# Attention and routed experts on one core: the last 64 key positions of the probabilities are transposed a turn later, inside the score tiles

## The chip, the cores and the metric

The kernel runs on one core of a Trainium2 chip. The time is device microseconds (us) from one launch, and fewer is better. A core has TensorE (PE in the profile, with its weight loads as PEld), VectorE (DVE), ScalarE (ACT), GpSimd (POOL) and SyncE (SP, which issues loads). They work side by side, each in the order in which its own instructions stand, and wait for each other through semaphores.

## What is computed

```python
def _attn_ref(q, k, v, tau):              # q, k, v: 8 batches x 8 heads x 576 x 64
    scores = q @ k.T / sqrt(64)
    scores = where(scores >= max(scores) - tau, scores, -1e9)
    attn = exp(scores - max(scores))
    attn = attn / (sum(attn) + 1e-9)
    return attn @ v

def _moe_ref(x, w_gate, w_output_gate, w1, w2):   # x: 4608 x 512, 8 experts of 1024
    e_idx = argmax(x @ w_gate)
    gate_w = softmax(x @ w_gate)[e_idx]
    eom = 1 / (1 + exp(-(x @ w_output_gate)))
    for e in range(8):
        mask = e_idx == e
        out[mask] = gate_w * eom[:, e] * (relu(x[mask] @ w1[e]) @ w2[e])
```

The attention output of all heads, put side by side, is the `x` of the experts. The change touches the attention alone.

## The kernel before, in words

The attention works in 32 units, each a pair of batches at one head. The two batches lie on the two halves of the 128 partitions. A unit has five turns `t` = 0 to 4 over the query rows: turns 0 to 3 take 128 queries of each batch (so two score tiles of 128 x 576), turn 4 takes the last 64 queries of both batches in one tile. `Attention.run` writes out the order of all engines by hand, turn after turn (`g` counts the turns of all units), and the scheduler is told to keep it on PE, DVE and ACT. A turn `g` works on several units of work at once:

- **scores** (L113 to L143): the score matmuls of turn `g` go to one or two `ps` tiles in PSUM, 1024 columns wide (two banks), of which columns 224 to 800 are used; columns 0 to 224 are free. DVE reads a `ps` tile with a running minimum and leaves `s` (L137). The pool has two `ps` tiles, so turn `g + 1` overwrites those of turn `g`.
- **x_rows** (L242 to L252, in turn 4 alone): small matmuls turn the unit before's output into rows, in the tiles `pr` and `pa`; ACT copies them out (L312).
- **exps** (L145 to L150): ACT makes `p` = exp(`s`), one instruction for each tile.
- **av_units** (L211 to L229): the product with `v` for the unit before, spread over turns 0 to 3 by the table `AV`. It reads the transposed probabilities `PTa` (turns 0 and 1 of its unit) and `PTb` (turns 2 to 4); its first matmuls of each half read block 8, the one that holds the last 64 key positions of both batches (the "remainder"). ACT copies the sums out (L228).
- **blocks** (L185 to L194): 16 transposes of `p` of turn `g - 2` to the tile `pt`, which ACT copies to `PTa` or `PTb` (L194). There is one `pt`. For a turn 4 it is **last_block** (L196 to L209) instead.
- **masks** (L152 to L166): DVE applies the threshold to `p` of turn `g - 1`.

The remainder of a turn's `p` has its own function, **remainder** (L168 to L183). In most turns it is two matmuls against the identity, 64 rows of `p` columns wide and 128 columns long, to a `pr` tile (L182), and one ACT copy (L183), right ahead of `blocks` and for the same turn `g - 2`:

```python
for pp in hs:
    o = M + pp.start
    nc.tensor.matmul(pr[pp, 0:P], p[:, o : o + 64], self.ident, start=True, stop=True)
nc.scalar.copy(PT[:, RB, q0 : q0 + P], pr[:, 0:P])
```

In a turn 4 that has `x_rows` it is a "pair" instead: two transposes of 64 rows (L177), one for each half of the queries, into columns of `pr` and `pa` that `x_rows` leaves free, and two ACT copies of 64 columns (L178).

Of the kernel before, what the change touches and what calls it, by code (L numbers as in the profile page):

```python
# [8 lines left out]
F32 = mybir.dt.float32  # L9
# [7 lines left out]
P = 128  # L17
# [3 lines left out]
class Attention:  # L21
    WU = 7
    SB = 4
    PB = 3
    LB = 3
    VB = 4
    WARM = {0: 4, 1: 2}
# [85 lines left out]
        self.load_qk(1)  # L113
        self.load_v(1)

    def scores(self, u, t):
        nc = self.nc
        q, k = self.loaded[u][0:2]
        S, HS = self.S, self.HS
        c0 = 512 - HS  # L120
        n = 2 if t < self.NB else 1
        ps = [self.ps_s.tile([P, 1024], F32, name="ps") for _ in range(n)]
        qs = q[:, t * P : t * P + P]
        for hf in range(2):
            for a in range(n):
                k0 = 0 if a else self.R
                pp = self.half[a] if n == 2 else slice(0, P)
                nc.tensor.matmul(  # L128
                    ps[a][:, c0 + hf * HS : c0 + hf * HS + HS], qs[pp], k[pp, k0 + hf * HS : k0 + hf * HS + HS],
                    start=True, stop=True,  # L130
                )
        mn = self.w3.tile([P, 2], F32, name="mn", bufs=4)
        ss = []
        SC = -(self.D ** -0.5)
        for a in range(n):
            s = self.sp.tile([P, S], F32, name="s", bufs=self.SB)
            nc.vector.tensor_scalar(  # L137
                s, ps[a][:, c0 : c0 + S], SC, None, op0=ALU.mult, op1=ALU.min, accum_out=mn[:, a : a + 1]
            )
            ss.append(s)  # L140
        thr = self.w3.tile([P, 2], F32, name="thr", bufs=4)
        self.router.gate = nc.gpsimd.tensor_scalar(thr[:, 0:n], mn[:, 0:n], self.tau, None, op0=ALU.add)  # L142
        return ss, mn, thr  # L143

    def exps(self, u, t, ss, mn, thr):  # L145
        p = self.sp.tile([P, 2 * self.S], F32, name="p", bufs=self.PB)
        for a, s in enumerate(ss):
            e = p[:, a * self.S : a * self.S + self.S]
            self.nc.scalar.activation(e, s, AF.Exp, bias=mn[:, a : a + 1], scale=-1.0)  # L149
        return p  # L150

    def masks(self, u, t, ss, mn, thr, p, between=None):  # L152
# [12 lines left out]
            nc.vector.tensor_copy(sums[:, 9:10], sums[:, 8:9])  # L165
            self.inverse(u)  # L166

    def remainder(self, u, t, p, pair=None):  # L168
        nc, hs, M, RB = self.nc, self.half, self.M, self.NK - 1
        if t == 0:  # L170
            self.PTa = self.w2.tile([P, self.NK, self.QA], F32, name="PTa")
        if t == 2:
            self.PTb = self.w2.tile([P, self.NK, self.S - self.QA], F32, name="PTb")
        PT, q0 = self.PTa if t < 2 else self.PTb, t % 2 * P
        if pair:
            for h in range(2):
                nc.tensor.transpose(pair[h], p[hs[h], M : M + P], self.ident[hs[h], hs[h]])  # L177
            return lambda h: nc.scalar.copy(PT[:, RB, q0 + 64 * h : q0 + 64 * h + 64], pair[h])  # L178
        pr = self.ps_r.tile([P, 512], F32, name="pr")
        for pp in hs:  # L180
            o = M + pp.start
            nc.tensor.matmul(pr[pp, 0:P], p[:, o : o + 64], self.ident, start=True, stop=True)  # L182
        nc.scalar.copy(PT[:, RB, q0 : q0 + P], pr[:, 0:P])  # L183

    def blocks(self, u, t, p):  # L185
        nc, id_, hs, RB = self.nc, self.ident, self.half, self.NK - 1
        PT, q0 = self.PTa if t < 2 else self.PTb, t % 2 * P
        pt = self.ps_t.tile([P, 1024], F32, name="pt")
        for b in range(RB):
            for h in range(2):  # L190
                o, k0 = h * 512 + b * 64, (b + b // 4) * P
                nc.tensor.transpose(pt[:, o : o + 64], p[hs[h], k0 : k0 + P], id_[hs[h], hs[h]])  # L192
        dst = PT[:, 0:RB, q0 : q0 + P].rearrange("p b (h j) -> p b h j", j=64)
        nc.scalar.copy(dst, pt.rearrange("p (h b j) -> p b h j", h=2, j=64))  # L194
# [93 lines left out]
    def run(self, hooks):  # L288
        nc, T, nu, rt = self.nc, self.NB + 1, self.nu, self.router
        G, W = nu * T, self.XW  # L290
        st, pr, av = {}, {}, {}
        self.prep_first()
        for g in range(G + T):
            u, t = divmod(g, T)
            if g < G:
                if t == 0 and u + 2 < nu:
                    self.load_qk(u + 2)
                    self.load_v(u + 2)
                st[g] = self.scores(u, t)
            if g in self.WARM:  # L300
                self.keep_warm(self.WARM[g])
            g2 = g - 2
            u2, t2 = divmod(g2, T)
            turn = 0 <= g2 < G
            xu = u - 1 if t == self.NB and u else None
            if xu is not None:
                ps = self.x_rows(xu)
                if turn:
                    out = self.remainder(u2, t2, pr[g2], [x[:, 5 * W : 5 * W + 64] for x in ps])
                xl = self.w2.tile([P, 2, 5, W], F32, name="xl")  # L310
                for a in (1, 0):
                    nc.scalar.copy(xl[:, a].rearrange("p j w -> p (j w)"), ps[a][:, 0 : 5 * W])  # L312
                    if turn:
                        out(a)
                self.x_out(xu, xl)
            if g < G:
                pr[g] = self.exps(u, t, *st[g])
            if t == 0 and u:
                av[u - 1] = self.av_units(u - 1)
            if u:  # L320
                for _ in range(*self.AV[t]):
                    next(av[u - 1])
            if turn:
                p = pr.pop(g2)
                if t2 == self.NB:
                    self.last_block(p)
                else:
                    if xu is None:
                        self.remainder(u2, t2, p)
                    self.blocks(u2, t2, p)  # L330
            if t == 1:
                rt.place(self.ps_r)
            g1 = g - 1
            if 0 <= g1 < G:
                self.masks(*divmod(g1, T), *st.pop(g1), pr[g1])
            if xu is not None:
                self.logits(xu, xl)
                if xu == nu - 1:
                    self.logit_sums(0)
                    self.logit_sums(1)  # L340
            if self.sumup and t in self.ROUTE:
                self.logit_sums(0 if t == self.ROUTE[0] else 1)
            if g in hooks:
                hooks[g]()
            rt.advance(t in self.ROUTE or u >= nu - self.H - 2)
# [301 lines left out]
class Experts:  # L647
    RB, NW, YB = 4, 4, 4
# [474 lines left out]
```

## Time and profile before

| what | value |
|---|---|
| median of 3 runs | 1011.85 us (1011.4 to 1012.84) |
| the profiled execution's own time | 1011.66 us |
| its span, first to last instruction | 1009.9 us |
| PE busy | 982.0 us (97% of the span) |
| DVE busy | 704.0 us (70%) |
| ACT busy | 604.5 us (60%) |
| POOL busy | 325.5 us (32%) |
| granted clock of TensorE, mean over the span | 0.993 |

The page's busy shares are means over two stages: the attention, to about 530 us, and the experts behind it. "Busy" of an instruction that is pipelined with its neighbours can be longer than the time by which it moves the next one, so the starts of neighbouring rows tell more than their durations. A weight load (PEld) is what waits on PE: a matmul's wait stands on its weight load.

### The profile page before, as it was taken

Reading aid. Unit: us, or ns where it says so; the run is one execution under the profiler, and the core shown is the slowest. Engines: PE = TensorE matmul, PEld = TensorE weight load, DVE = VectorE, ACT = ScalarE, POOL = GpSimd, SP = SyncE. Lnnn points to the kernel's source line nnn. Section 1 sums busy time; section 2 is a strip of 40 time slices with the busy share of each in tenths; the row PEclk is TensorE's granted clock in tenths of the full one; section 3 lists DMA queues with packets and bytes.
Section 4 is the critical chain, followed back from the end, with each engine's and each line's share of the span. In section 5 each row is a group of like instructions: output and inputs, shape, how many; then the busy total and the mean of one; then the engine's idle time right before and its main releaser. Section 6 shows DMA issues by size and latency. Waiting matters only on the chain. (4 is left out here: it accounts for less than half of the span.)

```text
span 1009.9 us, 21861 instructions
## 1 busy us (share of the span) xinstructions
PE 982.0 (97%) x8363; PEld 715.8 (71%) x8363; DVE 704.0 (70%) x1696; ACT 604.5 (60%) x1084; POOL 325.5 (32%) x617
## 2 busy tenths in 40 slices
PE   9999999999999999999989999999999999999894
PEld 5666666666666666666658888788878778778683
DVE  7898989899889998999876763435535436446621
ACT  6787887888887787778873432324424435336411
POOL 4344343454464556455536601102102002002101
PEclk9999999999999999999999999999999999999997
DMA  9962122121332114122216864335526526437201
GB/s 273 286 221 80 41 80 56 64 80 41 101 123 70 56 68 163 48 80 72 96 40 222 245 236 136 110 128 197 188 85 223 166 84 233 144 110 266 84 1 43
DMA packets 68843, 127.20 MB, mean 126 GB/s; under 512 B 6143, under 2 KB 32895, under 8 KB 68736
## 3 DMA queue, kind: packets, MB, share of 16 engines
q1 hardware_dynamic: 62096, 104.75, 33.0%
q0 software_dynamic: 6640, 21.02, 5.5%
q8 instruction: 67, 1.10, 0.5%
q14 instruction: 40, 0.33, 0.1%
HBM read 96.31 MB, written 30.22 MB: 125 GB/s over the span
## 5 line engine op out<-in xcount | busy, mean ns | idle before, releaser
L149 ACT ACTIVATE p<-s,mn 128x576 f32<-128x576 f32 x288 | 212.5, 783 | 53.8 <-DVE s L137 53.3
L137 DVE TENSOR_SCALAR_CACHE_REDUCE s<-ps 128x576 f32<-128x576 f32 x288 | 207.2, 752 | 36.2 <-PE ps L128 34.8
L159 DVE SCALAR_TENSOR_TENSOR p<-s,thr,p 128x576 f32<-128x576 f32 x288 | 225.3, 815 | 4.9 <-POOL thr L142 4.6
L128 PE MATMUL ps<-qk 64*128 64x288 f32 (+1 forms) x1152 | 198.7, 421 | 0.0
L907 ACT ACTIVATE hh<-ph 128x512 fp32r<-128x512 f32 (+2 forms) x96 | 48.8, 508 | 225.4 <-PE ph L904 219.5
L142 POOL TENSOR_SCALAR thr<-mn,tau_sb 128x2 f32<-128x2 f32 (+1 forms) x160 | 111.7, 698 | 214.1 <-DVE s L137 213.1
L908 DVE SCALAR_TENSOR_TENSOR hl<-ph,hh 128x512 fp32r<-128x512 f32 (+2 forms) x96 | 55.6, 579 | 164.5 <-ACT hh L907 162.0
L902 PE MATMUL ph<-xh,w1h 128*128 128x512 f32 (+2 forms) x384 | 136.5, 356 | 1.6 <-ACT xl L312 0.9
L903 PE MATMUL ph<-xl,w1h 128*128 128x512 f32 (+2 forms) x384 | 134.5, 350 | 3.0 <-DVE xl L732 2.2
L904 PE MATMUL ph<-xh,w1l 128*128 128x512 f32 (+2 forms) x384 | 133.4, 347 | 0.0
L128 PEld LDWEIGHTS ps<-qk 64*128 64x128 f32 (+1 forms) x1152 | 114.9, 189 | 22.1 <-DVE s L137 3.1
L720 POOL DMA_INDIRECT out_dram<-yo,kid x39 | 44.2, 1133 | 267.9 <-DVE yo L719 197.7
L926 PE MATMUL py<-w2h,hl 128*128 128x512 f32 x304 | 120.8, 397 | 1.0 <-DVE hl L908 1.0
L924 PE MATMUL py<-w2h,hh 128*128 128x512 f32 x304 | 120.5, 397 | 0.0
L925 PE MATMUL py<-w2l,hh 128*128 128x512 f32 x304 | 120.4, 396 | 0.0
L223 PE MATMUL pa<-PTb,vld 128*64 128x320 f32 x640 | 102.3, 447 | 1.0 <-ACT PTb L208 1.0
L192 PE MATMUL pt<-ident,p 64*128 64x64 f32 x2048 | 89.5, 227 | 3.6 <-ACT PTb L194 0.8
L192 PEld LDWEIGHTS pt<-ident,p 64*128 64x128 f32 x2048 | 73.6, 138 | 22.4 <-ACT PTb L194 10.8
L223 PE MATMUL pa<-PTa,vld 128*64 128x256 f32 x640 | 83.2, 389 | 0.3 <-ACT PTb L178 0.3
L903 PEld LDWEIGHTS ph<-xl,w1h 128*128 128x128 f32 x384 | 72.1, 188 | 15.8 <-DVE xl L732 6.0
L902 PEld LDWEIGHTS ph<-xh,w1h 128*128 128x128 f32 x384 | 72.1, 188 | 13.5 <-ACT xl L312 1.1
L732 DVE TENSOR_TENSOR w1l<-r,w1h 128x1024 fp32r<-128x1024 f32 x52 | 63.6, 1224 | 23.4 <-ACT w1h L729 22.9
(204 smaller groups left out, 1502.5 us busy)
## 6 DMA issues: line engine op xcount, KB each, us to landing
r<-in_moe_w_dram SPq DMA_DIRECT2D x104, 512.0 KB, 3.6
qk<-in_qkv_dram SPq DMA_DIRECT2D x31, 640.0 KB, 4.0
vld<-in_qkv_dram SPq DMA_DIRECT2D x32, 320.0 KB, 2.9
xs<-zrow SPq DMA_DIRECT2D x32, 257.0 KB, 8.0
xg<-xs SPq DMA_DIRECT2D x6, 1028.0 KB, 6.5
xg<-xs SPq DMA_DIRECT2D x4, 514.0 KB, 4.2
xg<-xs SPq DMA_DIRECT2D x2, 771.0 KB
out_dram<-yo,kid POOLq DMA_INDIRECT x39
```

The lines of the kernel that those rows point to most:

```text
L128: nc.tensor.matmul(ps[a][:, c0 + hf * HS : c0 + hf * HS + HS], qs[pp], k[pp, k0 + hf * HS : k0 + hf * HS + HS], start=True, stop=True,)
L137: nc.vector.tensor_scalar(s, ps[a][:, c0 : c0 + S], SC, None, op0=ALU.mult, op1=ALU.min, accum_out=mn[:, a : a + 1])
L149: self.nc.scalar.activation(e, s, AF.Exp, bias=mn[:, a : a + 1], scale=-1.0)
L159: nc.vector.scalar_tensor_tensor(e, s, thr[:, a : a + 1], e, op0=ALU.is_le, op1=ALU.mult, accum_out=sums[:, 2 * t + a : 2 * t + a + 1])
L192: nc.tensor.transpose(pt[:, o : o + 64], p[hs[h], k0 : k0 + P], id_[hs[h], hs[h]])
L223: nc.tensor.matmul(pa[self.half[a], 0:N], vm[:, kb, a], PT[:, 4 * a + kb if i else self.NK - 1], start=(i == 0), stop=(i == self.NB), skip ...
L902: nc.tensor.matmul(ph, w1h[:, c, fs], self.xh[:, c, 0:N], start=(c == 0), stop=False)
L903: nc.tensor.matmul(ph, w1h[:, c, fs], self.xl[:, c, 0:N], start=False, stop=False)
L904: nc.tensor.matmul(ph, w1l[:, c, fs], self.xh[:, c, 0:N], start=False, stop=(c == 3))
L924: nc.tensor.matmul(Y, hh[:, ts], wh, start=(f == 0), stop=False)
L925: nc.tensor.matmul(Y, hh[:, ts], wl, start=False, stop=False)
L926: nc.tensor.matmul(Y, hl[:, ts], wh, start=False, stop=(f == 7))
```

## The change

The remainder of every turn is now a pair of 64-row transposes, a turn later (of turn `g - 3` instead of `g - 2`). In a turn 4 with `x_rows` the pair still lies in `pr` and `pa`; in all other turns it goes to columns 0 to 64 of the turn's own two `ps` tiles, in front of the score matmuls, and its two ACT copies stand one ahead of each exp of that turn. The tiles of `PTa` and `PTb` are now taken by `blocks`. There are four `p` buffers instead of three. A turn whose `g - 3` is a turn 4 (that is `t` = 2) has no remainder.

```diff
-    PB = 3
+    PB = 4
...
-    def exps(self, u, t, ss, mn, thr):
+    def exps(self, u, t, ss, mn, thr, out=None):
         p = self.sp.tile([P, 2 * self.S], F32, name="p", bufs=self.PB)
         for a, s in enumerate(ss):
             e = p[:, a * self.S : a * self.S + self.S]
+            if out:
+                out(a)
             self.nc.scalar.activation(e, s, AF.Exp, bias=mn[:, a : a + 1], scale=-1.0)
...
-    def remainder(self, u, t, p, pair=None):
+    def remainder(self, u, t, p, pair):
         nc, hs, M, RB = self.nc, self.half, self.M, self.NK - 1
...
+        PT, q0 = self.PTa if t < 2 else self.PTb, t % 2 * P
+        for h in range(2):
+            nc.tensor.transpose(pair[h], p[hs[h], M : M + P], self.ident[hs[h], hs[h]])
+        return lambda h: nc.scalar.copy(PT[:, RB, q0 + 64 * h : q0 + 64 * h + 64], pair[h])
...
-        pr = self.ps_r.tile([P, 512], F32, name="pr")
-        for pp in hs:
-            o = M + pp.start
-            nc.tensor.matmul(pr[pp, 0:P], p[:, o : o + 64], self.ident, start=True, stop=True)
-        nc.scalar.copy(PT[:, RB, q0 : q0 + P], pr[:, 0:P])
...
+            g2, g3 = g - 2, g - 3
+            u3, t3 = divmod(g3, T)
+            late = 0 <= g3 < G and t3 < self.NB
...
+            if g < G or late and xu is None:
+                ps = [self.ps_s.tile([P, 1024], F32, name="ps") for _ in range(1 if t == self.NB and u else 2)]
+            if late and xu is None:
+                out = self.remainder(u3, t3, pr.pop(g3), [x[:, 0:64] for x in ps])
             if g < G:
...
+                st[g] = self.scores(u, t, ps)
...
             if g < G:
-                pr[g] = self.exps(u, t, *st[g])
+                pr[g] = self.exps(u, t, *st[g], out)
...
-                    if xu is None:
-                        self.remainder(u2, t2, p)
-                    self.blocks(u2, t2, p)
+                    self.blocks(*divmod(g2, T), pr[g2])
```

PE, from the `v` product of a turn 0 to that of turn 2, before (`PTa` and `PTb` are the transposed probabilities, `qk` the loaded queries and keys, `vld` the loaded values):

```order
L223 MATMUL pa<-PTa,vld 64x256 x4
L182 MATMUL pr<-ident,p 64x128 x2
L192 MATMUL pt<-ident,p 128x64 x16
L128 MATMUL ps<-qk 128x288 x4
L223 MATMUL pa<-PTa,vld 64x256 x6
L202 MATMUL pt<-ident,p 128x64 x2
L206 MATMUL pt<-ident,p 128x64 x8
L128 MATMUL ps<-qk 128x288 x4
L223 MATMUL pa<-PTb,vld 64x320 x4
L182 MATMUL pr<-ident,p 64x128 x2
L192 MATMUL pt<-ident,p 128x64 x16
```

The same place now, where the lines of scores, `v` product, blocks and last_block are L127, L220, L189, L199 and L203:

```order
L220 MATMUL pa<-PTa,vld 64x256 x4
L189 MATMUL pt<-ident,p 128x64 x16
L175 MATMUL ps<-ident,p 128x64 x2
L127 MATMUL ps<-qk 128x288 x4
L220 MATMUL pa<-PTa,vld 64x256 x6
L199 MATMUL pt<-ident,p 128x64 x2
L203 MATMUL pt<-ident,p 128x64 x8
L127 MATMUL ps<-qk 128x288 x4
L220 MATMUL pa<-PTb,vld 64x320 x4
L189 MATMUL pt<-ident,p 128x64 x16
L175 MATMUL ps<-ident,p 128x64 x2
```

Between the `v` product and the blocks nothing stands any more; the pair (L175) stands between the blocks and the scores of turns 1 and 3 (and of turn 0), and turn 2 has none.

PE again, now, with the semaphores that its instructions wait for (`Activation_49` counts ACT's instructions, `DVE_49` those of DVE), from the scores of a turn 0 to those of turn 1:

```order
L127 MATMUL ps<-qk 128x288 x3
L220 MATMUL pa<-PTa,vld 64x256 [waits DMAHW7_49,PE_49,Activation_49]
L220 MATMUL pa<-PTa,vld 64x256 x3
L189 MATMUL pt<-ident,p 128x64 [waits DVE_49,Activation_49]
L189 MATMUL pt<-ident,p 128x64 x7
L189 MATMUL pt<-ident,p 128x64 [waits DVE_49]
L189 MATMUL pt<-ident,p 128x64 x7
L175 MATMUL ps<-ident,p 128x64 [waits Activation_49] x2
L127 MATMUL ps<-qk 128x288 x4
```

Each of the two transposes of the pair waits for ACT: the first for turn 0's first copy, the second for its second copy, which read the columns that the pair overwrites. The scores stand behind them.

ACT, from the blocks' copy of a turn 4 (to `PTb`) to last_block's copies in turn 1, before:

```order
L194 COPY PTb<-pt 128x8x128 [waits PE_49]
L149 ACTIVATE p<-s,mn 128x576 [waits DVE_49] x2
L183 COPY PTb<-pr 128x128 [waits PE_49]
L194 COPY PTb<-pt 128x8x128 [waits PE_49]
L149 ACTIVATE p<-s,mn 128x576 [waits DVE_49] x2
L228 COPY X_206<-pa 128x256 [waits PE_49]
L208 COPY PTb<-pt 64x64 [waits PE_49]
L208 COPY PTb<-pt 64x64
L209 COPY PTb<-pt 128x8x64
```

And now (exp L150, pair's copy L176, blocks' copy L191, the `v` sums L225, last_block's first copy L205):

```order
L191 COPY PTb<-pt 128x8x128 [waits PE_49,Activation_49]
L176 COPY PTb<-ps 128x64 [waits DVE_49]
L150 ACTIVATE p<-s,mn 128x576
L176 COPY PTb<-ps 128x64 [waits DVE_49]
L150 ACTIVATE p<-s,mn 128x576
L191 COPY PTb<-pt 128x8x128 [waits PE_49]
L176 COPY PTb<-ps 128x64 [waits DVE_49]
L150 ACTIVATE p<-s,mn 128x576
L176 COPY PTb<-ps 128x64 [waits DVE_49]
L150 ACTIVATE p<-s,mn 128x576
L225 COPY X_205<-pa 128x256 [waits PE_49]
L205 COPY PTb<-pt 64x64 [waits PE_49]
```

One copy of 128 columns behind two exps has become two copies of 64 columns, one ahead of each exp, and each copy waits for DVE, which reads the same `ps` tile (L136 now, L137 before).

## Rows read from the trace of the kernel before

**Rows 1.** The page's first two parts: busy time of each engine, and the granted clock of TensorE in 40 equal slices of the span, in tenths (9 is 90% or more).

```profile
PE 982.0 (97%) x8363; PEld 715.8 (71%) x8363; DVE 704.0 (70%) x1696; ACT 604.5 (60%) x1084; POOL 325.5 (32%) x617
...
PEclk9999999999999999999999999999999999999997
```

**Rows 2.** Busy time by stretches: 31 to 514 us (30 units of the attention), its drain to 530 us, and the experts. Columns: stretch: its length, busy us (instructions) of PE, PEld, DVE, ACT and POOL, granted clock, share of the DMA engines, GB/s.

```profile
31.00:514.00 483.00, 479.54 (x5540) 312.86 (x5537) 438.68 (x1264) 394.11 (x760) 229.74 (x407) 1.00 0.29 92
514.00:530.00 16.00, 12.68 (x160) 8.59 (x159) 9.40 (x19) 11.14 (x23) 4.34 (x7) 1.00 0.22 57
530.00:1010.00 480.00, 460.21 (x2427) 377.93 (x2425) 232.60 (x347) 178.87 (x271) 78.20 (x107) 0.99 0.46 153
```

**Rows 3.** The timeline of PE's weight loads over one unit's length, from the scores of a turn 4 to those of the next. Columns: start, length, engine, line, operation, out<-in, shape, count, and in brackets the idle time before it with what ended it. Of `x_rows` (L249) the first row alone is shown, and the first blocks are left out.

```profile
350.97 0.78 PEld L128 LDWEIGHTS ps<-qk 128*128 128x128 f32 x4
352.14 0.18 PEld L249 LDWEIGHTS pr<-wx,X 64*128 64x128 f32 x1 [0.39 <-ACT PTa L194]
...
353.81 0.80 PEld L128 LDWEIGHTS ps<-qk 64*128 64x128 f32 x8
355.00 0.63 PEld L223 LDWEIGHTS pa<-PTa,vld 128*64 128x64 f32 x8 [0.38 <-ACT PTb L178]
355.70 0.36 PEld L182 LDWEIGHTS pr<-ident,p 128*64 128x64 f32 x4
356.39 0.57 PEld L192 LDWEIGHTS pt<-ident,p 64*128 64x128 f32 x16 [0.34 <-ACT PTb L194]
356.88 0.79 PEld L128 LDWEIGHTS ps<-qk 64*128 64x128 f32 x8
358.06 1.06 PEld L223 LDWEIGHTS pa<-PTa,vld 128*64 128x64 f32 x12 [0.38 <-issue]
359.51 0.14 PEld L202 LDWEIGHTS pt<-ident,p 64*128 64x128 f32 x2 [0.38 <-issue]
...
359.81 0.79 PEld L128 LDWEIGHTS ps<-qk 64*128 64x128 f32 x8
361.06 0.20 PEld L223 LDWEIGHTS pa<-PTb,vld 128*64 128x64 f32 x4 [0.45 <-ACT PTb L208]
361.67 0.20 PEld L223 LDWEIGHTS pa<-PTb,vld 128*64 128x64 f32 x4 [0.41 <-ACT PTb L209]
361.99 0.41 PEld L182 LDWEIGHTS pr<-ident,p 128*64 128x64 f32 x4
362.57 0.58 PEld L192 LDWEIGHTS pt<-ident,p 64*128 64x128 f32 x16 [0.17 <-PE pa L223]
363.06 0.79 PEld L128 LDWEIGHTS ps<-qk 64*128 64x128 f32 x8
364.24 1.27 PEld L223 LDWEIGHTS pa<-PTb,vld 128*64 128x64 f32 x12 [0.38 <-issue]
365.64 0.41 PEld L182 LDWEIGHTS pr<-ident,p 128*64 128x64 f32 x4
366.23 0.57 PEld L192 LDWEIGHTS pt<-ident,p 64*128 64x128 f32 x16 [0.17 <-issue]
366.87 0.78 PEld L128 LDWEIGHTS ps<-qk 128*128 128x128 f32 x4
```

**Rows 4.** The timeline of ACT in the same unit, from the pair's copies in turn 4 to last_block's copy in turn 1, and the copy of the `v` sums in turn 3.

```profile
354.04 0.22 ACT L178 COPY PTb<-pa 128x64 f32<-128x64 f32 x1
354.15 0.51 ACT L312 COPY xl<-pr 128x400 f32<-128x400 f32 x1
354.53 0.24 ACT L178 COPY PTb<-pr 128x64 f32<-128x64 f32 x1
354.63 0.81 ACT L149 ACTIVATE p<-s,mn 128x576 f32<-128x576 f32 x1
355.31 1.03 ACT L194 COPY PTb<-pt 128x1024 f32<-128x1024 f32 x1
356.20 1.48 ACT L149 ACTIVATE p<-s,mn 128x576 f32<-128x576 f32 x2
357.55 0.29 ACT L183 COPY PTb<-pr 128x128 f32<-128x128 f32 x1
357.69 1.06 ACT L194 COPY PTb<-pt 128x1024 f32<-128x1024 f32 x1
358.97 1.45 ACT L149 ACTIVATE p<-s,mn 128x576 f32<-128x576 f32 x2 [0.22 <-DVE s L137]
360.33 0.35 ACT L228 COPY X<-pa 128x256 f32<-128x256 f32 x1
...
361.03 0.58 ACT L209 COPY PTb<-pt 128x512 f32<-128x512 f32 x1
...
366.51 0.41 ACT L228 COPY X<-pa 128x320 f32<-128x320 f32 x1
```

**Rows 5.** The timeline of DVE in the same unit: the second reading of turn 0's score tiles, and the first of turn 1's.

```profile
355.78 0.75 DVE L137 TENSOR_SCALAR_CACHE_REDUCE s<-ps 128x576 f32<-128x576 f32 x1
...
358.17 0.76 DVE L137 TENSOR_SCALAR_CACHE_REDUCE s<-ps 128x576 f32<-128x576 f32 x1 [0.24 <-PE ps L128]
```

**Rows 6.** The waits of PE's weight loads from 31 to 514 us. Columns: who waited, for whom: us in total, times, longest.

```profile
PEld pa L223 <- ACT PTb L209: 11.6, 30, 0.4
...
PEld pt L192 <- ACT PTb L194: 9.8, 29, 0.3
```

More of the change, by code (lines that the diff above doesn't have):

```diff
@@ L114, in prep_first, with scores @@
         self.load_v(1)
-    def scores(self, u, t):
+    def scores(self, u, t, ps):
         nc = self.nc
@@ L121, in scores @@
         n = 2 if t < self.NB else 1
-        ps = [self.ps_s.tile([P, 1024], F32, name="ps") for _ in range(n)]
         qs = q[:, t * P : t * P + P]
@@ L148, in exps @@
             e = p[:, a * self.S : a * self.S + self.S]
+            if out:
+                out(a)
             self.nc.scalar.activation(e, s, AF.Exp, bias=mn[:, a : a + 1], scale=-1.0)
+        if out and len(ss) == 1:
+            out(1)
         return p
@@ L166, in masks, with blocks @@
             self.inverse(u)
-    def remainder(self, u, t, p, pair=None):
+    def remainder(self, u, t, p, pair):
         nc, hs, M, RB = self.nc, self.half, self.M, self.NK - 1
+        PT, q0 = self.PTa if t < 2 else self.PTb, t % 2 * P
+        for h in range(2):
+            nc.tensor.transpose(pair[h], p[hs[h], M : M + P], self.ident[hs[h], hs[h]])
+        return lambda h: nc.scalar.copy(PT[:, RB, q0 + 64 * h : q0 + 64 * h + 64], pair[h])
+    def blocks(self, u, t, p):
+        nc, id_, hs, RB = self.nc, self.ident, self.half, self.NK - 1
         if t == 0:
@@ L173, in remainder @@
             self.PTb = self.w2.tile([P, self.NK, self.S - self.QA], F32, name="PTb")
[L174 to L178, printed above, removed]
-        pr = self.ps_r.tile([P, 512], F32, name="pr")
-        for pp in hs:
-            o = M + pp.start
-            nc.tensor.matmul(pr[pp, 0:P], p[:, o : o + 64], self.ident, start=True, stop=True)
-        nc.scalar.copy(PT[:, RB, q0 : q0 + P], pr[:, 0:P])
-    def blocks(self, u, t, p):
-        nc, id_, hs, RB = self.nc, self.ident, self.half, self.NK - 1
         PT, q0 = self.PTa if t < 2 else self.PTb, t % 2 * P
@@ L294, in run @@
             u, t = divmod(g, T)
+            if g < G and t == 0 and u + 2 < nu:
+                self.load_qk(u + 2)
+                self.load_v(u + 2)
+            g2, g3 = g - 2, g - 3
+            u3, t3 = divmod(g3, T)
+            late = 0 <= g3 < G and t3 < self.NB
+            xu = u - 1 if t == self.NB and u else None
+            out = None
+            ps = []
+            if g < G or late and xu is None:
+                ps = [self.ps_s.tile([P, 1024], F32, name="ps") for _ in range(1 if t == self.NB and u else 2)]
+            if late and xu is None:
+                out = self.remainder(u3, t3, pr.pop(g3), [x[:, 0:64] for x in ps])
             if g < G:
[L296 to L299, printed above, removed]
+                st[g] = self.scores(u, t, ps)
+            elif out:
+                out(0)
+                out(1)
             if g in self.WARM:
                 self.keep_warm(self.WARM[g])
[L302 to L305, printed above, removed]
             if xu is not None:
-                ps = self.x_rows(xu)
-                if turn:
-                    out = self.remainder(u2, t2, pr[g2], [x[:, 5 * W : 5 * W + 64] for x in ps])
+                px = self.x_rows(xu)
+                if late:
+                    out = self.remainder(u3, t3, pr.pop(g3), [x[:, 5 * W : 5 * W + 64] for x in px])
                 xl = self.w2.tile([P, 2, 5, W], F32, name="xl")
                 for a in (1, 0):
-                    nc.scalar.copy(xl[:, a].rearrange("p j w -> p (j w)"), ps[a][:, 0 : 5 * W])
-                    if turn:
+                    nc.scalar.copy(xl[:, a].rearrange("p j w -> p (j w)"), px[a][:, 0 : 5 * W])
+                    if late:
                         out(a)
+                out = None
                 self.x_out(xu, xl)
             if g < G:
-                pr[g] = self.exps(u, t, *st[g])
+                pr[g] = self.exps(u, t, *st[g], out)
             if t == 0 and u:
@@ L322, in run @@
                     next(av[u - 1])
[L323 to L326, printed above, removed]
-                else:
-                    if xu is None:
-                        self.remainder(u2, t2, p)
-                    self.blocks(u2, t2, p)
+            if 0 <= g2 < G:
+                if g2 % T == self.NB:
+                    self.last_block(pr.pop(g2))
+                else:
+                    self.blocks(*divmod(g2, T), pr[g2])
             if t == 1:
```

## Prediction

> **What bounds the kernel now.** I read the busy shares first, then the stretches, then one unit's timeline on PE, and last what PE waits for. PE is busy for 97% of the span at full clock [rows 1]. In the attention it is 479.5 of 483 us, with DVE at 438.7 and ACT at 394.1, and the experts behind it are PE's too [rows 2]. So what is added to or taken from PE's line in a unit moves the end, one for one, unless PE sits waiting there. The reader should therefore look for PE's own waits inside a unit. The unit shown takes 366.87 - 350.97 = 15.90 us and has two places where ACT holds PE [rows 3]: the blocks of turn 0 start at 356.39, behind ACT's copy of the blocks of turn 4, which ends at 355.31 + 1.03 = 356.34 [rows 3, 4]; and the second half of turn 2's `v` product starts at 361.67, behind last_block's copy that ends at 361.61 [rows 3, 4]. Both recur in nearly all of the 30 units, 29 and 30 times [rows 6]. PE goes on about 0.05 us after ACT's end.
>
> Other short pauses of PE are no waits for anyone: where it goes over from the `v` product (columns of the array split) to transposes (rows split) the next load starts late. That pause is 0.17 us behind matmuls of 128 columns (L182) and 0.38 behind those of 256 (L223 to L202) [rows 3].
>
> **The change, part by part.** I follow the shown unit, with the new times beside the old.
>
> *Turn 0, L182 goes.* The `v` product's loads end at 355.63; with a pause of 0.38 the blocks could start at 356.02 instead of 356.39 (with the pair that now stands in front of turn 0's scores, at 356.08). But ACT's copy still ends at 356.34: its chain, from `x_rows` over two row copies, two pair copies and one exp, stays as it was. The blocks start at 356.39 as before. Gain: 0. This is the first place where saved PE time has no taker.
>
> *Turn 1, the pair waits.* Its second transpose may start when turn 0's second copy has been read out, as the order of PE shows. On ACT the instruction behind the blocks' copy starts at 356.20 [rows 4]; that is now the first copy. A 64-column copy takes 0.22 to 0.24 us, but the next instruction starts 0.10 to 0.11 behind it (354.04 to 354.15, 354.53 to 354.63) [rows 4]. So the exp starts at 356.30. Two exps take from 356.20 to 357.55, 0.675 each [rows 4], so the second copy starts at 356.98 and ends at 357.22. DVE's second reading of `ps` ends at 356.53 [rows 5] and does not come last. PE goes on at 357.27, and with a transpose of 0.03 (16 blocks move PE by 356.88 - 356.39 = 0.49 [rows 3], so 0.06 for a pair) the scores start at 357.31 instead of 356.88: **+0.43 us**. Queued behind the waiting transpose on PE are the scores, and DVE waits for these.
>
> *Turn 1 on ACT.* DVE already waited for these scores (0.24 us [rows 5]) and ACT for DVE (0.22 [rows 4]), so both move by 0.43. Each of the two exps now has a copy ahead of it, 0.10 each. The first cannot hide in ACT's wait, since it waits for DVE's reading of the same tile as the exp does. ACT runs on without a pause to last_block's copy [rows 4], which thus ends 0.43 + 0.20 = 0.63 later, and PE waited for it: turn 2's second half starts at 361.67 + 0.63 = 362.30.
>
> The Trainium skill, page "PSUM — Partial Sum Buffer", section "PSUM bank collisions raise a hardware error", says that two engines must not touch the same bank and quadrant at once, two readers included, which speaks against putting ACT's data into DVE's tile; the order's waits agree. Without that rule the first copy would hide in ACT's 0.22 us wait, and the sum would be 0.10 us per unit smaller.
>
> *Turn 2, L182 goes and nothing comes.* Before, the blocks start at 362.57, which is 0.70 behind the end of the `v` product's loads (361.87). Now only the pause is left. For matmuls of 320 columns no row shows it alone: by the two rows, 0.17 at 128 and 0.38 at 256 columns, it grows by 0.107 per 64 columns, so 0.49; the lower bound is the 0.38 of 256 columns itself. I take 0.49, since the row's own trend has to go on. Loads end at 362.50, blocks start at 362.99 instead of 362.57: **+0.42**.
>
> *Turn 3, pair in, L182 out.* The pair adds 0.06: scores at +0.48. Its `ps` tiles are free, since turn 2 has no copies. The `v` product's loads end at 365.51 + 0.48 = 365.99; blocks at 366.48 instead of 366.23 (0.72 has become 0.49): **+0.25**. The scores of turn 4 follow at +0.25.
>
> *Nothing else takes it back.* `x_rows` starts 1.17 us behind those scores (350.97 to 352.14 [rows 3]), so at 368.29 the next time, and needs ACT's sums from turn 3; these end at 366.51 + 0.41 = 366.92 [rows 4] and will end at most 0.48 + 0.20 later, at 367.60. The pair in turn 4 is the old one with another turn's data. No DMA, and nothing on SP or POOL, is moved. The fourth `p` buffer only costs memory. ACT gains six copies of 0.10 and loses three of 0.14 to 0.16 in a unit (357.55 to 357.69 [rows 4]), some 0.15 us, all of it at the places above.
>
> **Sum.** +0.25 us in each of 30 units is 7.5 us; first unit and drain nothing that I can tell. The profiled execution took 1011.66 us (span 1009.9), 0.19 under the median of the runs, so I forecast 1011.66 + 7.5 = **1019.2 us**, 0.7% slower. About 2 us, 0.2%, is what a measurement here can tell from no change.
>
> **The rivals.**
>
> *Balance.* If the pause behind 320 columns is 0.38 like that behind 256, turns 2 and 3 each give back 0.11 more: +0.03 to +0.04 a unit, +1.2 us, 1012.9 us. For it: 0.38 also stands behind the score matmuls of 288 columns (the load of 358.06) [rows 3], which the trend would put higher. Against it: the same columns split as at 128 and 256, where it grew.
>
> *Copies that hand over later.* If a copy out of `ps` holds ACT for 0.14 us, as the 128-column copy does (357.55 to 357.69 [rows 4]), turn 1's scores come at +0.47 and last_block's copy at +0.75, so +0.37 a unit: +11 us, 1022.8 us. With no overlap at all (0.24 each) it would be +0.57, +1.05 and +0.67: +20 us, 1031.8 us, the upper bound. Against it: two rows with 64 columns show 0.10 to 0.11.
>
> The Trainium skill, page "ScalarE: Activation LUTs", section "What ACT_TABLE_LOAD costs", gives 186 ns plus 0.833 ns per element for an instruction with immediate scale and bias, and an overlap of 93 ns; its estimate for 64 columns is 0.24 us and a hand-over of 0.146. The trace agrees with the first and shows 0.10 for the second. By the page the sum would be that of this rival.
>
> *The other side: ACT out of the way.* What makes it slower is one copy's end at 357.22. If it has ended by 356.86, before PE has the blocks of turn 0 out, PE does not wait. That takes ACT 0.36 us earlier at turn 0, by a blocks' copy or a chain from `x_rows` that runs shorter than in the row. Then turn 1's scores come at +0.06, last_block's copy at +0.26, turn 2's blocks at +0.05 and turn 3's at -0.12: -3.6 us, 1008.1 us; with turn 1's copies hidden as well -0.32 a unit and 1002 us. For it: PE's own work does fall, by 0.21 and 0.23 in turns 2 and 3. Against it: ACT works without a pause from 354.04 on up to the second copy [rows 4], and PE waited for that very chain 29 times [rows 6].
>
> *That it does not do what it says* is excluded by the order of PE and ACT.
>
> **How the numbers follow.** Forecast as summed 0.62, late hand-over 0.10, balance 0.15, ACT out of the way 0.13. The range goes from 1012 (below the balance) to 1028 us (most of the way to copies that do not overlap); it leaves out the faster case and the last of the upper bound, 0.18 together. Faster by over 0.2% is 0.13, within 0.2% is the balance, 0.15, slower 0.72.
>
> **What would show it.** In the changed profile a load of L175 in turn 1 should wait for ACT's L176 some 30 times, and scores of turn 1 start about 6.3 us behind those of turn 4 instead of 5.9. The blocks of turn 0 should still wait for L191, now with a longer idle time. Behind the `v` product of turns 2 and 3 the blocks (L189) should start 0.49 us after its last load. A unit should take 16.15 us. Wrong would be: no wait of L175 for ACT, a pause of 0.38, copies that hold ACT for 0.2, or a unit of 15.8 us.

## The result, and the profile after

The changed kernel takes **1020.66 us** (median of 4 runs, 1019.59 to 1021.49), the kernel before beside it 1012.35 (4 runs): a ratio of 1.0082, 95% interval [1.0065, 1.01]. The profiled execution took 1019.88 us, its span is 1018.2, 8.2 us longer than before. So it is slower, by about what the sum said (1019.2).

The page's first two parts after:

```profile
PE 976.5 (96%) x8169; PEld 707.0 (69%) x8169; DVE 705.7 (69%) x1696; ACT 611.2 (60%) x1181; POOL 326.2 (32%) x617
...
PEclk9999999999999999999999999999999999999997
```

PE has 194 instructions and 5.5 us of work less than in [rows 1], at the same granted clock (0.992, before 0.993), and the span is longer: PE waits more. ACT has 97 instructions and 6.7 us more. Where PE waits, its weight loads show, here from 31 to 520 us (who waited, for whom: us in total, times, longest):

```profile
PEld pt L189 <- issue: 27.4, 56, 0.5
...
PEld pt L189 <- ACT PTb L191: 20.0, 29, 0.7
...
PEld pa L220 <- ACT PTb L206: 12.1, 30, 0.4
...
PEld ps L175 <- ACT PTb L176: 9.5, 32, 0.6
```

The old waits of [rows 6] are still there: for last_block's copy 30 times as before, and the blocks of turn 0 still wait for ACT 29 times, now 20.0 us in all instead of 9.8, since PE comes there earlier. New is the last row, a wait of the pair's transposes for ACT's copies. The first is a pause ahead of the blocks, 0.49 us each time where [rows 3] has 0.17. One unit's PE timeline, from the scores of a turn 4 to the next (columns as in [rows 3]; `x_rows`, the first blocks and some rows of turns 1 and 2 left out):

```profile
357.78 0.78 PEld L127 LDWEIGHTS ps<-qk 128*128 128x128 f32 x4
...
360.63 0.15 PEld L175 LDWEIGHTS ps<-ident,p 64*128 64x128 f32 x2
360.69 0.80 PEld L127 LDWEIGHTS ps<-qk 64*128 64x128 f32 x8
361.87 0.63 PEld L220 LDWEIGHTS pa<-PTa,vld 128*64 128x64 f32 x8 [0.39 <-ACT PTa L176]
363.19 0.58 PEld L189 LDWEIGHTS pt<-ident,p 64*128 64x128 f32 x16 [0.69 <-ACT PTb L191]
363.68 0.14 PEld L175 LDWEIGHTS ps<-ident,p 64*128 64x128 f32 x1
364.08 0.14 PEld L175 LDWEIGHTS ps<-ident,p 64*128 64x128 f32 x1 [0.26 <-ACT PTb L176]
364.08 0.84 PEld L127 LDWEIGHTS ps<-qk 64*128 64x128 f32 x8
365.31 1.06 PEld L220 LDWEIGHTS pa<-PTa,vld 128*64 128x64 f32 x12 [0.38 <-issue]
...
369.06 0.20 PEld L220 LDWEIGHTS pa<-PTb,vld 128*64 128x64 f32 x4 [0.41 <-ACT PTb L206]
369.74 0.57 PEld L189 LDWEIGHTS pt<-ident,p 64*128 64x128 f32 x16 [0.49 <-issue]
370.24 0.14 PEld L175 LDWEIGHTS ps<-ident,p 64*128 64x128 f32 x2
370.30 0.79 PEld L127 LDWEIGHTS ps<-qk 64*128 64x128 f32 x8
371.47 1.27 PEld L220 LDWEIGHTS pa<-PTb,vld 128*64 128x64 f32 x12 [0.39 <-issue]
373.24 0.57 PEld L189 LDWEIGHTS pt<-ident,p 64*128 64x128 f32 x16 [0.49 <-issue]
373.88 0.78 PEld L127 LDWEIGHTS ps<-qk 128*128 128x128 f32 x4
```

And ACT in the same unit, from the blocks' copy of turn 4 on:

```profile
362.10 1.03 ACT L191 COPY PTb<-pt 128x1024 f32<-128x1024 f32 x1
362.99 0.26 ACT L176 COPY PTb<-ps 128x64 f32<-128x64 f32 x1
363.10 0.83 ACT L150 ACTIVATE p<-s,mn 128x576 f32<-128x576 f32 x1
363.78 0.25 ACT L176 COPY PTb<-ps 128x64 f32<-128x64 f32 x1
363.87 0.83 ACT L150 ACTIVATE p<-s,mn 128x576 f32<-128x576 f32 x1
...
366.15 0.21 ACT L176 COPY PTb<-ps 128x64 f32<-128x64 f32 x1 [0.55 <-DVE s L136]
...
368.42 0.59 ACT L206 COPY PTb<-pt 128x512 f32<-128x512 f32 x1
```

The unit takes 373.88 - 357.78 = 16.10 us; the median of all 31 distances between scores of turn 4 is the same, against 15.89 before. Counted from the unit's first row, by place (predicted shift beside the measured one):

| place | before | after | shift | predicted |
|---|---|---|---|---|
| blocks of turn 0 start | 5.42 | 5.41 | 0 | 0 |
| scores of turn 1 start | 5.91 | 6.30 | +0.39 | +0.43 |
| last_block's copy ends | 10.64 | 11.23 | +0.59 | +0.63 |
| blocks of turn 2 start | 11.60 | 11.96 | +0.36 | +0.42 |
| scores of turn 3 start | 12.09 | 12.52 | +0.43 | +0.48 |
| scores of turn 4 start | 15.90 | 16.10 | +0.20 | +0.25 |

The 8.2 us of span are made up of these: 31 times 0.207 (the median unit) is 6.4; the first scores of turn 4 come 0.5 later (16.24 against 15.71); all 31 distances together exceed 31 medians by 6.5 instead of 5.0, which is 1.5; and what follows the last of these scores is 0.2 shorter (496.3 against 496.5).

### The profile page after: what moved, and what is told of

The parts are those of the page before. It is cut to its first block, busy times and chain, and to the rows that moved or that the text cites. A ratio compares the mean times of both kernels' runs of the same rounds, so it can differ in the third digit from the quotient of the medians.

```text
span 1018.2 us, 21662 instructions
## 1 busy us (share of the span) xinstructions
PE 976.5 (96%) x8169; PEld 707.0 (69%) x8169; DVE 705.7 (69%) x1696; ACT 611.2 (60%) x1181; POOL 326.2 (32%) x617
## 5 line engine op out<-in xcount | busy, mean ns | idle before, releaser
L136 DVE TENSOR_SCALAR_CACHE_REDUCE s<-ps 128x576 f32<-128x576 f32 x288 | 207.5, 753 | 41.7 <-PE ps L127 40.0
L150 ACT ACTIVATE p<-s,mn 128x576 f32<-128x576 f32 x288 | 222.6, 790 | 16.3 <-DVE s L136 13.6
L127 PE MATMUL ps<-qk 64*128 64x288 f32 (+1 forms) x1152 | 202.6, 423 | 0.5 <-ACT PTb L176 0.5
L127 PEld LDWEIGHTS ps<-qk 64*128 64x128 f32 (+1 forms) x1152 | 123.6, 190 | 15.6 <-DVE s L136 1.5
L189 PEld LDWEIGHTS pt<-ident,p 64*128 64x128 f32 x2048 | 74.1, 138 | 53.8 <-issue 28.8
L220 PE MATMUL pa<-PTb,vld 128*64 128x320 f32 x640 | 102.3, 447 | 1.3 <-ACT PTb L205 0.9
L189 PE MATMUL pt<-ident,p 64*128 64x64 f32 x2048 | 90.1, 227 | 7.9 <-ACT PTb L191 7.3
L220 PE MATMUL pa<-PTa,vld 128*64 128x256 f32 x640 | 83.2, 389 | 0.7 <-ACT PTa L176 0.7
```

What stands on the lines that cost most here:

```text
L127: nc.tensor.matmul(ps[a][:, c0 + hf * HS : c0 + hf * HS + HS], qs[pp], k[pp, k0 + hf * HS : k0 + hf * HS + HS], start=True, stop=True,)
L136: nc.vector.tensor_scalar(s, ps[a][:, c0 : c0 + S], SC, None, op0=ALU.mult, op1=ALU.min, accum_out=mn[:, a : a + 1])
L220: nc.tensor.matmul(pa[self.half[a], 0:N], vm[:, kb, a], PT[:, 4 * a + kb if i else self.NK - 1], start=(i == 0), stop=(i == self.NB), skip ...
```

## The experiments

Below, "unit" is the median distance between the scores of two turns 4, from the profile of the run. Line numbers move by a few from kernel to kernel. The times are medians. The ratios stand to the kernel before, run on the same chip; they are estimated from all runs and need not be the quotient of two medians.

**1. Both copies behind both exps** (the wait made longer)

```diff
         for a, s in enumerate(ss):
             ...
-            if out:
-                out(a)
             self.nc.scalar.activation(e, s, AF.Exp, bias=mn[:, a : a + 1], scale=-1.0)
-        if out and len(ss) == 1:
+        if out:
+            out(0)
             out(1)
```

> The changed kernel with both pair copies behind the two exps of their turn, instead of one ahead of each; same instructions, other order on ACT. Queue theory (mine: what costs is PE's wait in turn 1 for the END of turn 0's second copy): the second copy of turn 0 now ends 0.65 us later (two exps of 0.68 us ahead of both), so turn 1's scores come 1.05 us later than before the change instead of 0.39, last_block's copy 1.25 later, and a unit takes about 16.75 us: some +26 us on before, about 1038 us. Rival A (the transposes in front of the scores cost PE itself): as the change, 1020 us. Rival B (six ACT copies in place of three, wherever they stand): as the change, 1020 us.

Measured: 1058.99 us, 1.0464 [1.0449, 1.048]; unit 17.39 (16.75 expected). The waits of its weight loads from 31 to 520 us:

```profile
PEld ps L174 <- ACT PTb L175: 25.5, 28, 1.6
...
PEld ps L127 <- ACT PTb L175: 16.8, 28, 0.6
```

With the same instructions as the changed kernel, the place of the copies on ACT alone, two in each of turns 0, 1 and 3, is worth 38 us. The first wait came as expected: turn 1's scores start at 6.96, 1.05 later than before. The second was not expected: turn 2's scores (10.64) now wait 0.62 us for turn 1's copies, which release the score tiles that they write. Turn 4's scores wait for turn 3's copies in the same way, mostly for 0.17 us. I had followed the pair in turn 1 only, and the same tie to ACT exists in each turn that has a pair.

**2. Turn 0: both copies ahead of the first exp** (the wait taken away, all instructions kept)

```diff
-            if out:
+            if out and t == 0:
+                if a == 0:
+                    out(0)
+                    out(1)
+            elif out:
                 out(a)
```

> The changed kernel with both copies ahead of the first exp in turn 0 alone; same instructions. Queue theory: turn 0's second copy ends 0.45 us earlier, at about 5.85 us of the unit, as early as PE has the blocks out; PE's wait in turn 1 goes, its scores come at +0.03 instead of +0.39, last_block's copy at +0.23, and a unit takes 15.76 us: 4 us under before, about 1008 us. Rivals A and B: 1020 us, since neither the transposes nor the number of copies change.

Measured: unit 15.78 as expected (15.76); 1012.32 us, 1.0003 [0.9993, 1.0012], not as expected. Its waits from 31 to 520 us, and the pair of turn 1:

```profile
PEld ps L179 <- ACT PTb L180: 2.6, 9, 0.5
```

```profile
358.83 0.17 PEld L179 LDWEIGHTS ps<-ident,p 64*128 64x128 f32 x2
358.89 0.82 PEld L127 LDWEIGHTS ps<-qk 64*128 64x128 f32 x8
```

Of 32 waits 9 are left, and in the unit shown (from 352.93) the pair is a single row of two and turn 1's scores start at 5.96. The unit is 0.33 shorter with all transposes and all six copies in it. So neither the transposes nor ACT's added work in turn 0 cost these 0.33: it is the moment at which the second copy ends. (ACT's added work in turn 1 does cost, as experiment 4 shows.) The time is lower by 8 us as well, but doesn't fall below that of before, though the unit does by 0.12. The end of this section comes back to that.

**3. and 4. No copies in turn 0, or in turn 1**

The copies are left out, and GpSimd writes zeros where ACT would put them.

```diff
+    def blank(self, t):
+        PT, q0 = self.PTa if t < 2 else self.PTb, t % 2 * P
+        self.nc.gpsimd.memset(PT[:, self.NK - 1, q0 : q0 + P], 0.0)
...
+                if u and t == 0:          # 4: t == 1
+                    self.blank(t3)
...
-                pr[g] = self.exps(u, t, *st[g], out)
+                pr[g] = self.exps(u, t, *st[g], None if u and t == 0 else out)
```

> The changed kernel without the two ACT copies of turn 0 (left out: GpSimd writes zeros to these columns of PTb instead, ahead of its other work in the turn); the transposes stay. Queue theory: as with both copies first, PE's wait in turn 1 goes: 15.76 us a unit, about 1008 us. Rival A: 1020 us. Rival B: a third of what six copies cost comes back, the same as when turn 1's copies are left out.

Measured: unit 15.77; 1011.51 us, 0.9996 [0.9985, 1.0006].

> The changed kernel without the two ACT copies of turn 1 (left out: GpSimd writes zeros to these columns of PTb instead); the transposes stay. Queue theory: PE's wait in turn 1 for turn 0's copy stays (scores at +0.39), but last_block's copy comes only 0.39 later and not 0.59: a unit takes 15.90 us, about 1012.5 us, as before. So this gives back 0.2 us a unit and turn 0's copies 0.34. Rival A: 1020 us. Rival B: the same gain as without turn 0's copies.

Measured: unit 15.89, turn 1's scores still at 6.30; 1018.31 us, 1.0057 [1.0039, 1.0076].

Both units came within 0.01 of what was expected. Without turn 0's copies all of 0.33 goes, as in the second experiment. Without turn 1's, 0.21 goes, all of it from last_block's copy on, which ends at 11.02 instead of 11.22 (medians): the 0.20 that the sum gave to the two copies on ACT. Both times missed what was expected (1008 and 1012.5). In experiment 4 the profiled execution (1014.92) was quicker than the median, GpSimd has work added, and one unit took 19.23 us.

**5. and 6. The kernel before without L182 and L183, in turn 0, or in turns 2 and 3**

They are left out, and GpSimd writes zeros there, too.

```diff
-                    if xu is None:
+                    if xu is None and not (u and t == 0):     # 6: t in (2, 3)
                         self.remainder(u2, t2, p)
+                    elif xu is None:
+                        self.fresh(t2)
```

> The kernel before the change without turn 0's remainder (left out: two matmuls L182 and the copy L183; GpSimd writes zeros in their place). Queue theory: PE's time that this frees has no taker, since the blocks of turn 0 wait for ACT's copy of turn 4's blocks: no change, 1012.4 us, and the idle time ahead of turn 0's blocks grows from 0.34 to 0.69 us. Rival (PE's work counts wherever it is taken away): 0.37 us a unit, -11 us, 1001 us.

Measured: unit 15.90, the blocks of turn 0 still at 5.43, behind a wait of 0.78 instead of 0.34; 1013.44 us, 1.0013 [1.0003, 1.0023]. The wait from 31 to 514 us, 9.8 us in [rows 6]:

```profile
PEld pt L200 <- ACT PTb L202: 22.8, 30, 0.8
```

> The kernel before the change without the remainders of turns 2 and 3 (left out, GpSimd writes zeros in their place). Queue theory: there PE itself is what is waited for, and each turn gives back 0.22 us (0.70 to 0.72 between the v product's last load and the blocks becomes 0.49): 15.45 us a unit, -14 us, 998.5 us. Rival (removing L182 is worth little, it hides in the pause of PE): within 2 us of 1012.4.

Measured: unit 15.47; 1002.98 us, 0.991 [0.9895, 0.9925]. Its pause ahead of the blocks is 0.49 us in both turns; the blocks of turn 2 start 0.21 earlier than before (11.39), those of turn 3 0.43 (14.82).

The same two instruction groups are worth nothing in turn 0 and 0.43 us a unit in turns 2 and 3, where PE, ahead of the blocks, waits for nothing but itself. This is the price of the work, and what the change could have gained at most there. The unit came out right both times; of 13.3 us (31 times 0.43) the medians show 8.9 (1011.87 for the kernel before in these runs), where 998.5 us was expected.

**7. DVE copies, ahead of its reading of the scores** (turn 4's pair left on ACT)

```diff
-        return lambda h: nc.scalar.copy(PT[:, RB, q0 + 64 * h : q0 + 64 * h + 64], pair[h])
+        copy = nc.vector.tensor_copy if dve else nc.scalar.copy
+        return lambda h: copy(PT[:, RB, q0 + 64 * h : q0 + 64 * h + 64], pair[h])
...
             s = self.sp.tile([P, S], F32, name="s", bufs=self.SB)
+            if out:
+                out(a)
             nc.vector.tensor_scalar(
```

> The changed kernel with the pair copies out of the score tiles made by DVE, each ahead of DVE's own reading of that tile, instead of by ACT; turn 4's pair stays on ACT. Queue theory: DVE waits for the scores in turns 1 and 3 anyway and its reading ends before PE is back, so PE's wait in turn 1 goes and nothing stands ahead of the exps: scores of turn 1 at +0.03, last_block's copy at +0.03, a unit at 15.55 us, -10 us on before, about 1002 us. Rival (DVE, busy for 91% of the attention, becomes the bound): six copies of 0.1 us or more a unit on it, 1015 us or more.

Measured: unit 15.91; 1017.58 us, 1.0053 [1.0041, 1.0066]. Turn 1 in its timeline:

```profile
345.04 1.27 PE L127 MATMUL ps<-qk 64*128 64x288 f32 x8
...
346.06 0.22 DVE L237 RECIPROCAL rinv<-rinv 128x10 f32<-128x10 f32 x1
346.31 0.22 DVE L181 COPY PTb<-ps 128x64 f32<-128x64 f32 x1
346.46 0.75 DVE L138 TENSOR_SCALAR_CACHE_REDUCE s<-ps 128x576 f32<-128x576 f32 x1
347.13 0.08 DVE L138 DVE_READ_ACCUMULATOR s<-ps 128x1 f32 x1
347.13 0.22 DVE L181 COPY PTb<-ps 128x64 f32<-128x64 f32 x1
347.25 1.58 ACT L154 ACTIVATE p<-s,mn 128x576 f32<-128x576 f32 x2 [0.65 <-DVE s L138]
347.27 0.75 DVE L138 TENSOR_SCALAR_CACHE_REDUCE s<-ps 128x576 f32<-128x576 f32 x1
```

The expectation failed at one step. I had let the copies hide in DVE's wait for the scores of turn 1, 0.24 us in [rows 5], since the pair is done before the scores. But each copy takes 0.14 to 0.15 us of DVE (346.31 to 346.46, 347.13 to 347.27), and the two of turn 0 use that wait up: DVE is free at 346.28 (346.06 + 0.22), and the scores end at 346.31 (345.04 + 1.27). So the two copies of turn 1 come on top. The copy can't start before the scores end, either: PE writes both into one tile, and the copy waits for all that PE puts there. In the shown turn that is worth 0.03 us, in turn 3 up to 0.27. What DVE waited for in front of its copies, over the whole run:

```profile
its engine sat idle before it (us, times) until:
  PE ps L127: 3.3, 13
```

Turn 1's scores do start early (6.04), but the exps 0.25 later than before (8.25 against 8.00), and last_block's copy ends 0.37 later; that alone brings the unit back to 15.91.

**8. All pairs by DVE, turn 4's in its score tile too**

```diff
+                pair = [ps[0][:, 0:64], ps[1][:, 0:64] if len(ps) > 1 else ps[0][:, 960:1024]]
+                out = self.remainder(u3, t3, pr.pop(g3), pair, True)
...
                 px = self.x_rows(xu)
-                if late:
-                    out = self.remainder(u3, t3, pr.pop(g3), [x[:, 5 * W : 5 * W + 64] for x in px])
```

> As with DVE's copies, and turn 4's pair also goes to the free columns of its one score tile (0 to 64 and 960 to 1024) and is copied by DVE, so that ACT's chain from x_rows to the copy of turn 4's blocks loses two copies and waits for no transposes behind x_rows. Queue theory: that chain is what turn 0's blocks wait for; it ends 0.28 us earlier, so does turn 0: a unit at 15.27 us, -19 us on before, about 993.5 us. Rival (DVE becomes the bound): slower than with turn 4's pair on ACT.

Measured: unit 16.15; 1021.04 us, 1.0088 [1.0075, 1.0101]. PE's loads in turn 1, DVE's work that they wait for, and a wait from 31 to 520 us:

```profile
348.50 0.57 PEld L194 LDWEIGHTS pt<-ident,p 64*128 64x128 f32 x16 [0.51 <-ACT PTb L196]
348.99 0.14 PEld L179 LDWEIGHTS ps<-ident,p 64*128 64x128 f32 x1
349.54 0.13 PEld L179 LDWEIGHTS ps<-ident,p 64*128 64x128 f32 x1 [0.40 <-PE pt L194]
```

```profile
348.54 0.21 DVE L181 COPY PTb<-ps 128x64 f32<-128x64 f32 x1
348.67 0.74 DVE L140 TENSOR_SCALAR_CACHE_REDUCE s<-ps 128x576 f32<-128x576 f32 x1
349.35 0.08 DVE L140 DVE_READ_ACCUMULATOR s<-ps 128x1 f32 x1
```

```profile
PE ps L179 <- DVE s L140: 12.4, 34, 0.9
```

ACT is relieved and the blocks of turn 0 start at 5.15, 0.27 earlier than before. But now DVE's second reading of turn 0's tiles ends last (348.67 + 0.74 = 349.41, and PE goes on at 349.54), and the load of turn 1's pair waits 0.40 us. The wait has changed hands and is longer than the 0.26 of the changed kernel. The profile puts the load's idle time down to PE's own blocks (L194); but in turn 3 of the same unit the pair follows the same blocks without a wait (355.29 to 355.78), the tile that the second transpose writes is the one that DVE's reading empties, and the last row has the transposes themselves, not only their loads, waiting for that reading 34 times.

**9. and 10. Two mixed versions**

Both leave turn 1 without a pair: turn 3's remainder of the unit before is done in the old way (two matmuls into `pr`, one copy) in front of its blocks in turn 0, where PE waits anyway. The ninth has the second experiment's order of copies in addition, the tenth that of the change.

```diff
-            late = 0 <= g3 < G and t3 < self.NB
+            late = 0 <= g3 < G and t3 < self.NB - 1
...
+                    if g2 % T == self.NB - 1:
+                        self.whole(pr[g2])
                     self.blocks(*divmod(g2, T), pr[g2])
```

> The changed kernel with both copies ahead of the first exp in turn 0, and with the remainder that was turned in front of turn 1's scores done as before the change: two matmuls to a pr tile in turn 0, ahead of the blocks, and one ACT copy behind turn 0's exps; so turn 1 has no pair and no copies. Queue theory: the two matmuls lie in PE time of turn 0 that has no taker (leaving them out of the kernel before changed nothing), nothing waits in turn 1, and the gains of turns 2 and 3 (0.22 each) stay, less 0.03 to 0.06 for each pair: a unit at 15.55 us (15.89 before, 16.10 with the change). Over the units without routing that is -8 us; the units with routing gave none of such gains back so far, so about 1004 us. Rival (PE's own work counts wherever it stands): the two matmuls and their pause cost turn 0 0.37 us a unit against both copies first (15.77), 16.1 us a unit, 1015 us or more.

Measured: unit 15.69; 1011.7 us (1004 expected), 0.9993 [0.9983, 1.0003]. Turn 2's `v` product waits for last_block's smaller copies for 0.61 us, where it paused for 0.45 [rows 3]:

```profile
347.48 0.20 PEld L232 LDWEIGHTS pa<-PTb,vld 128*64 128x64 f32 x4 [0.61 <-ACT PTb L217]
```

> The same, but in turn 0 one copy ahead of each exp, as in the change. Queue theory: the second copy again ends at about 6.25 us of the unit; there is no pair to hold up all scores of turn 1, but those of the second batch overwrite the tile and wait for it, 0.15 to 0.2 us: a unit at 15.69 us, some 3 us slower than with both copies first. Rival (the order of copies and exps is of no matter once turn 1 has no pair): the same as with both first.

Measured: unit 15.75; 1012.02 us, 1.0003 [0.9993, 1.0014].

Both units are shorter than that of before, by 0.20 and 0.14, and neither time can be told from it. No version here that computes everything beats the kernel before.

**11. The changed kernel again**

> The changed kernel once more, beside the two above on one chip: 16.10 us a unit and 1020 us, by each theory.

Measured: 1019.59 us, 1.0079 [1.0066, 1.0092]; unit 16.09.

**Where the units' gains go.** The first scores of a turn 4 and all that follows the last differ by some us from execution to execution, without order. What grows is the excess: what the 31 distances of a profile have in all over 31 times their median. The last two columns are of the 18th unit alone, explained below.

| kernel | unit, us | excess, us | profiled time | ratio | 18th unit over the median | GpSimd idle there |
|---|---|---|---|---|---|---|
| before | 15.89 | 5.0 | 1011.66 | 1 | 0.0 | 3.4 |
| changed | 16.10 | 6.5 | 1019.88 | 1.0082 | 1.3 | 4.9 |
| changed, again | 16.09 | 6.9 | 1019.59 | 1.0079 | 1.3 | 4.9 |
| experiment 1 | 17.39 | 4.6 | 1059.56 | 1.0464 | 0.0 | 2.9 |
| experiment 2 | 15.78 | 9.4 | 1012.26 | 1.0003 | 2.2 | 5.1 |
| experiment 3 | 15.77 | 8.2 | 1012.08 | 0.9996 | 2.3 | 5.0 |
| experiment 4 | 15.89 | 9.3 | 1014.92 | 1.0057 | 1.4 | 4.4 |
| experiment 5 | 15.90 | 7.1 | 1011.8 | 1.0013 | 1.5 | 4.3 |
| experiment 6 | 15.47 | 10.7 | 1002.85 | 0.991 | 2.0 | 4.8 |
| experiment 7 | 15.91 | 9.8 | 1016.68 | 1.0053 | 1.5 | 4.3 |
| experiment 8 | 16.15 | 9.3 | 1022.71 | 1.0088 | 1.0 | 4.0 |
| experiment 9 | 15.69 | 11.3 | 1009.89 | 0.9993 | 2.1 | 5.1 |
| experiment 10 | 15.75 | 13.6 | 1017.11 | 1.0003 | 2.5 | 5.6 |

Most of the excess lies among the 17th to 20th and the 25th to 31st unit, in which GpSimd also puts routed tokens where they belong. The waits in the 18th unit of the changed kernel, 290.3 to 307.7 us:

```profile
POOL LX L468 <- DMA xs<-rows,dsti: 4.9, 1, 4.9
...
DVE p L162 <- POOL thr L141: 1.8, 1, 1.8
...
PEld ps L127 <- ACT PTb L176: 1.1, 2, 0.6
```

GpSimd stands behind a scatter for 4.9 us; DVE's masks wait for the thresholds that GpSimd computes next (1.8), and PE, at the end of that chain, for a copy (1.1). In the kernel before GpSimd is idle at the same place, behind the same scatter, for 3.4 us (the profile puts that down to DVE), and nothing waits for the thresholds:

```profile
POOL LX L464 <- DVE s L137: 3.4, 1, 3.4
```

The last two columns go together in all rows: 2.9 and 3.4 us of idle time leave the 18th unit at its median, 4.0 us and more make it 1.0 to 2.5 us longer. The trace of the transfers has the reason for the longer idle time, one step further back: the scatter's data starts to move 1.8 us after its issue in the kernel before and in experiment 1, and 2.9 to 4.1 us after it in all others. Why it starts later there stays open.

In size the excess fits what is missing: in experiment 2 the units give 31 times 0.12, or 3.7 us, and the excess takes 4.4 more than before; in the sixth they give 13.3 and it takes 5.7. But it is not the price of shorter units: experiments 4, 5, 7 and 8 have units as long as that of before, or longer, and an excess of 7.1 to 9.8. Nor is it steady, since there is one profile of a kernel, two of the changed one: that of experiment 10 took 5.1 us more than the median of its runs, that of experiment 4 3.4 us less. So where the gains go is shown, into these units; what sends them there is shown for the 18th only, and up to the late scatter.

## Why the prediction was right

**The bound.** PE in the attention, with its waits for ACT, was the right place to look. Experiment 5 shows that PE's work in front of a wait is worth 0, experiment 6 that it is worth its full length where there is none.

**Turn 0.** A gain of 0 was forecast and measured; the wait for L191 grew from 0.34 to 0.69 us, and took all that PE saved there.

**Turn 1.** The second copy was to end at 6.25 in the unit; it ends at 363.78 + 0.25 - 357.78 = 6.25. The load goes on 0.05 later, as forecast. The 0.04 that the term was too high is at the end of it: the scores' first load starts together with the second pair's load (both at 364.08), where I had charged a transpose of 0.03 in between; the rest is a slip of addition (357.27 and 0.03 make 357.30, not 357.31). All later places are too high by this 0.04 to 0.06 and no more. Experiments 2 and 3 take the wait away and with it 0.33 of the unit.

**Turn 1 on ACT.** The two copies held ACT for 0.20 by the sum: 0.59 - 0.39 after, and 0.21 of the unit in experiment 4. That the first copy can't hide in ACT's wait is borne out: it starts at 366.15, after an idle time of 0.55, just behind the end of DVE's reading of the same tile (365.35 + 0.76 = 366.11):

```profile
365.35 0.76 DVE L136 TENSOR_SCALAR_CACHE_REDUCE s<-ps 128x576 f32<-128x576 f32 x1 [0.56 <-PE ps L127]
```

The Trainium skill's rule (page "PSUM — Partial Sum Buffer", section "PSUM bank collisions raise a hardware error") forbids two engines in one bank and quadrant at once; all copies here keep to it, because the kernel's order makes them, so no run shows what a collision does. Experiment 7 shows a further tie that I had missed: the copy waits for the scores in its tile as well.

**Turn 2 and turn 3.** The pause behind 320 columns, which no row showed alone, is 0.49 as the trend gave; the balance's 0.38 falls.

**Late hand-over** falls: the copies hand over after 0.11, 0.09 (362.99 to 363.10, 363.78 to 363.87), not 0.14. The estimate of 0.146, worked out from what the Trainium skill (page "ScalarE: Activation LUTs", section "What ACT_TABLE_LOAD costs") gives for an ACTIVATE, is not what this trace shows for a copy.

**ACT out of the way** did not come about, but its mechanism is right: experiment 2 makes the copy end early, and the unit falls by 0.12, as that rival had it. The 1008.1 us it gave did not come: 1012.32. The step that failed there is the last, 30 units times the gain: the excess of the long units took 4.4 us back, for reasons that are known in part only.

**The sum.** 0.207 instead of 0.25 a unit, in 31 distances instead of 30, is 6.4 where the sum had 7.5 us; the start and the routing units, for which it had nothing, add 2.0, and the end takes 0.2. Of these 2.0 the 18th unit alone has 1.3, through the late scatter, which no part of the sum foresaw. So the mechanism gave 6.4 of the 8.2 us, and that the sum came within 2 us is in part luck: small errors of opposite sign.

## What to carry to other kernels

Work taken from an engine is worth what the wait behind it leaves: look first at which engine ends last at that place, and move work off the stretches in which nothing is waited for. Data put into the free columns of another engine's tile shares that tile's whole life: its copy waits for everything written there, and the tile is released by the slower of its readers, so ask where in the reader's queue the copy stands, since the same copies, one ahead of each exp or both behind the two exps, differed by 38 us here. A gain per unit measured in the typical unit has to be looked for again in the units in which another engine leads.

## What the runs showed of the hardware

- In the units shown, a copy of 128x64 out of `ps` takes 0.21 to 0.23 us on DVE and holds it for 0.11 to 0.15 (experiments 7 and 8); on ACT it takes 0.20 to 0.26 and holds it for 0.09 to 0.11 (the changed kernel). So the engine that I took for the freer one pays more for each copy.
- Behind one and the same scatter of rows GpSimd's next instruction stood idle for 2.9 to 5.6 us in thirteen profiles. From 4.0 us on DVE's masks waited 0.5 to 2.6 us for the thresholds that GpSimd computes next, and the unit was 1.0 to 2.5 us longer.
- The pause of PE ahead of the transposes is longer the more columns the matmuls before it have: 0.17 us at 128, 0.38 at 256 [rows 3], 0.49 at 320 (56 times).
